# An expert mixture per unit of 128 tokens, and a rearranged beginning, in a fused linear-attention and mixture kernel

## The chip, the cores and the metric

The kernel runs on one core of a Trainium2 chip. The metric is the device time of one launch in microseconds (us), as the median of several launches. Engines: PE is TensorE (matmuls), PEld its loads of stationary operands, DVE is VectorE, ACT is ScalarE, POOL is GpSimd, SP is SyncE, which in this kernel does nothing but issue DMA transfers. L504 is line 504 of the kernel in question; the changed kernel has other line numbers than the one before.

## The reference, cut to what matters

```python
# attention: 4 batches, 8 heads, 768 steps, head size 40, float32
for t in range(S):
    y[:, :, t] = einsum('bhd,bhde->bhe', rt, state)
    Sa = einsum('bhde,bhe->bhd', state, at)
    state_decay = state * wt[:, :, None, :] - einsum('bhd,bhe->bhde', Sa, bt)
    state = state_decay + einsum('bhd,bhe->bhde', vt, kt)
# y becomes x: 3072 tokens of 320 values. Mixture of 4 experts, F = 1024:
for e in range(E):
    h = maximum(x @ w1[e], 0.0)
    out += p[:, e:e + 1] * (h @ w2[e])       # p: domain_probs, normalized per token
```

## The kernel before

The recurrence is done in 12 chunks of 64 steps. Two batches of a chunk make a unit of 128 tokens, so there are 24 units: 0 and 1 are the first chunk, 2 and 3 the second, and so on. For each unit the kernel loads six inputs (W, A, B, K, V, R) and then has four stages:

- `within`: everything that needs no state. TensorE transposes the inputs and multiplies them; VectorE copies the results through a causal mask (for instance the scores of V and R, into `CT`).
- `substitute`: a forward substitution in 31 steps of two instructions each, on VectorE for units 0 and 1 and on GpSimd for the others.
- `merge`: the substitution's result is turned into `Qc`, `QTc` and `QT`.
- `step`: state update and the unit's output, matmuls `py` on TensorE, `Y` on VectorE. Twelve small DMA transfers then rearrange Y to `xT`, the moving operand of the mixture.

The mixture is cut into pieces, and after each stage one piece is placed, so that TensorE has work while the chain of small operations waits. Python generators express this; a scheduler then settles the order on each engine, and each engine runs its instructions in that order.

```python
def mixture(c, xT):                    # c: a chunk, so 256 tokens = two units
    def up(e, quad):                   # half an expert: 16 + 8 matmuls of 256 columns
        for f in range(4):
            for g in range(2):
                nc.tensor.matmul(out=ph[f % 2][:, f // 2, :],
                    lhsT=w1_sb[:, e, g, (f0 + f) * P:(f0 + f + 1) * P], rhs=xT[:, g, :], ...)
        ...                            # w_last: rows 256 to 319 of w1, on half the array
        nc.scalar.activation(out=h[:], in_=ph[i][:], func=ACTF.Relu)
    def down(e, s):                    # one expert for one unit: 8 matmuls of 320 columns
        ...
# ... (order at the start)
load(0)                                # SyncE: inputs of unit 0
run(within(units[0]))
substitute(units[0], nc.vector)
load(1)
load_experts()                         # SyncE: gates and all weights
run(within(units[1]))
first_merge = merge(units[0]); run(first_merge, 2)
substitute(units[1], nc.vector)
for u in range(NU):
    ...
    load(u + 2)                        # SyncE
    ...
    if n == 6 and more:
        substitute(units[u + 2], nc.gpsimd)
    mix(1)                             # one piece of mixture
    if q.bp == B // 2 - 1:             # after every second unit
        work.append(mixture(q.c, xT))
```

## Time and profile before

| kernel before | |
|---|---|
| time, median of the first 3 launches | 1286.18 us (1285.4 to 1286.84) |
| profiled launch, span and mean granted clock | 1286.0 us, 0.965 |
| TensorE busy | 1201.8 us (93%) |
| first mixture matmul | 122.6 us |
| period of a unit in the steady part | 49.46 us |

The prediction below shows the lines of this profile and reads them: about 160 us at the beginning, and the full part behind them.

### The profile page before, as it was taken

What the parts mean: (1) busy time and instruction counts of PE and PEld (TensorE: products, weight loads), DVE (VectorE), ACT (ScalarE), POOL (GpSimd) and SP (SyncE); (2) the same over time, 40 slices, a digit from 0 to 9 for tenths busy, and PEclk for the clock granted to TensorE, in tenths of its full rate; (3) what the DMA queues carried; (4) which work ended last, traced back from release to release, by engine and by line L of the source; (5) the groups of instructions that cost most, each with busy time, mean ns of one, the idle gap of its engine ahead of it and who ended that gap; (6) DMA issues with size and microseconds to landing.
All of it is one profiled execution on the core that took longest, in us unless ns stands there. A gap on an engine that the chain in (4) does not pass through costs nothing.

```text
span 1286.0 us, 38173 instructions
## 1 busy us (share of the span) xinstructions
PE 1201.8 (93%) x16416; PEld 928.3 (72%) x16416; DVE 403.6 (31%) x854; ACT 320.8 (25%) x801; POOL 474.0 (37%) x1601
## 2 busy tenths in 40 slices
PE   4454799999999999999999999999999999999998
PEld 3443677777777777777777777777777777777776
DVE  6853223233143143143142232232331431411000
ACT  2121222232222222322222222232222222222111
POOL 2025632633534524525425426326335345240000
PEclk8656899999999999999999999999999999999999
DMA  4941111121120220220220220210211201000000
GB/s 63 319 71 26 29 31 31 23 36 21 30 39 14 37 39 12 39 39 10 41 38 10 42 35 10 44 31 11 47 22 19 47 16 27 14 13 2 17 1 11
DMA packets 182200, 45.27 MB, mean 35 GB/s; under 512 B 162576, under 2 KB 181008, under 8 KB 182032
## 3 DMA queue, kind: packets, MB, share of 16 engines
q1 hardware_dynamic: 182032, 42.83, 17.2%
q8 instruction: 130, 2.13, 0.7%
q14 instruction: 38, 0.31, 0.1%
HBM read 34.13 MB, written 3.93 MB: 30 GB/s over the span
## 4 chain that ended last, share of the span: by engine, by line
PE 88%; POOL 3%; ACT 2%; DVE 2%; SPq 2%; issue 2%; DMA 1%; DVEq 0%; ACTq 0%
PE po L505 33%; PE ph L487 26%; PE ph L493 8%; PE py L240 2%; PE psd L240 2%; SPq L157 2%; POOL Z L338 1%; POOL tmp L334 1%; PE pc L240 1%; PE pf L240 1%; PE psa L240 1%; PE px L240 1%; PE psn L240 1%; ACT QT L377 1%; PE pY L360 1%
## 5 line engine op out<-in xcount | busy, mean ns | idle before, releaser
L505 PE MATMUL po<-w_sb,hs 128*128 128x320 f32 x1536 | 441.9, 439 | 0.0
L505 PEld LDWEIGHTS po<-w_sb,hs 128*128 128x128 f32 x1536 | 282.5, 190 | 112.5 <-issue 3.6
L487 PE MATMUL ph<-xT,w_sb 128*128 128x256 f32 x1536 | 355.5, 384 | 0.0
L487 PEld LDWEIGHTS ph<-xT,w_sb 128*128 128x128 f32 x1536 | 286.3, 191 | 39.4 <-issue 0.3
L334 POOL TENSOR_TENSOR tmp<-M,Z 128x60 f32<-128x60 f32 (+24 forms) x682 | 188.7, 277 | 97.2 <-DVE M L327 45.5
L338 POOL TENSOR_TENSOR Z<-Z,tmp 128x60 f32<-128x60 f32 (+24 forms) x682 | 194.0, 285 | 53.4
L499 ACT ACTIVATE hs<-ph 128x512 f32<-128x512 f32 x192 | 104.3, 595 | 395.1 <-PE ph L493 395.1
L322 POOL COPY blocks<-F 32x256 f32<-32x256 f32 x88 | 34.7, 394 | 385.1 <-ACT F L303 382.4
L513 DVE SCALAR_TENSOR_TENSOR osb<-po,gate,osb 128x320 f32<-128x320 f32 x72 | 39.6, 551 | 249.9 <-PE po L505 249.9
L493 PE MATMUL ph<-xT,w_last 64*128 64x256 f32 x768 | 108.9, 402 | 0.0
L493 PEld LDWEIGHTS ph<-xT,w_last 64*128 64x128 f32 x768 | 66.1, 186 | 36.1 <-issue 31.8
L248 DVE COPY_PREDICATED TT<-mask_up,px 128x256 f32<-128x256 int32 x48 | 18.7, 438 | 192.2 <-PE px L240 192.2
L248 DVE COPY_PREDICATED TT<-mask_up,pe 128x256 f32<-128x256 int32 x48 | 18.6, 438 | 135.1 <-PE pe L240 135.1
L259 ACT COPY G<-pw 128x504 f32<-128x504 f32 x24 | 13.9, 580 | 188.5 <-DVE Y L461 150.8
L327 DVE STREAM_TRANSPOSE M<-blocks 128x1024 f32<-128x1024 f32 x24 | 46.8, 1951 | 33.0 <-POOL blocks L322 32.9
L330 POOL COPY Z<-unit_cols 128x256 f32<-128x256 f32 x22 | 8.8, 398 | 122.0 <-DVE Qc L345 122.0
L273 DVE RECIPROCAL gp<-gp 128x320 f32<-128x320 f32 x24 | 51.4, 2143 | 0.0
L315 ACT COPY EV<-pev 64x160 f32<-64x160 f32 x96 | 22.9, 286 | 101.1 <-PE pev L240 100.9
L353 POOL COPY QT<-QTc 32x256 f32<-32x256 f32 x96 | 40.1, 417 | 14.3 <-DVE QTc L347 7.6
L213 PE MATMUL pg<-ident,G 128*128 128x128 f32 x96 | 17.6, 311 | 29.2 <-DVE G L260 29.2
L511 DVE TENSOR_SCALAR osb<-po,gate 128x320 f32<-128x320 f32 x24 | 13.2, 551 | 91.1 <-PE po L505 91.1
L283 ACT COPY AT<-pAT 128x512 f32<-128x512 f32 x24 | 14.1, 586 | 107.9 <-PE pAT L213 107.9
(111 smaller groups left out, 1200.0 us busy)
## 6 DMA issues: line engine op xcount, KB each, us to landing
w_sb<-in_moe_w_dram SPq DMA_DIRECT2D x4, 1280.0 KB
w_sb<-in_moe_w_dram SPq DMA_DIRECT2D x8, 512.0 KB
natW<-in_w_dram SPq DMA_DIRECT2D x48, 80.0 KB
natA<-in_a_dram SPq DMA_DIRECT2D x48, 80.0 KB
natB<-in_b_dram SPq DMA_DIRECT2D x48, 80.0 KB
natK<-in_k_dram SPq DMA_DIRECT2D x48, 80.0 KB
out_dram<-osb SPq DMA_DIRECT2D x48, 80.0 KB
xT<-Y SPq DMA_DIRECT2D x168, 20.0 KB
```

Source lines behind the costliest of these rows:

```text
L240: nc.tensor.matmul(out=p[row][half(col), at * out_cols:(at + 1) * out_cols], lhsT=lhsT, rhs=rhs, start=(n == 0), stop=(n == len(terms) - 1),)
L248: nc.vector.copy_predicated(out=of_slot(m[:], s), mask=mask_up[:, None, :].to_broadcast([P, NJ, L]), data=p[s],)
L273: nc.vector.reciprocal(out=gp[:], in_=gp[:])
L327: nc.vector.transpose(out=M[:], in_=cols)
L334: eng.tensor_tensor(out=t, in0=M[:, j:j + 1, j + 1:Q].to_broadcast([P, n, m]), in1=Z[:, 0:n, j:j + 1].to_broadcast([P, n, m]), op=ALU.mult,)
L338: eng.tensor_tensor(out=Z[:, 0:n, j + 1:Q], in0=Z[:, 0:n, j + 1:Q], in1=t, op=ALU.add)
L353: ins = nc.gpsimd.tensor_copy(out=q.QT[quarter(i), :, quarter(i % 2)], in_=QTc[quarter(i)])
L487: nc.tensor.matmul(out=ph[f % 2][:, f // 2, :], lhsT=w1_sb[:, e, g, (f0 + f) * P:(f0 + f + 1) * P], rhs=xT[:, g, :], start=(g == 0 and f < ...
L493: nc.tensor.matmul(out=ph[i][:, f // 2, :], lhsT=w1_last[i * DT:(i + 1) * DT, e, (f0 + f) // 2, :], rhs=xT[i * DT:(i + 1) * DT, 2, :], sta ...
L499: nc.scalar.activation(out=h[:], in_=ph[i][:], func=ACTF.Relu)
L505: nc.tensor.matmul(out=po[:], lhsT=hs[e, f // 4, f % 2][:, f % 4 // 2, s * P:(s + 1) * P], rhs=w2_sb[:, e, f, :], start=(f == 0), stop=(f ...
L513: nc.vector.scalar_tensor_tensor(out=osb[s][:], in0=po[:], scalar=sc, in1=osb[s][:], op0=ALU.mult, op1=ALU.add,)
```

## The change

The diff says it in its title: the mixture works on one unit of 128 tokens, with whole experts as pieces; the first two units are interleaved; their loads are split over two queues; and the weights come through GpSimd's queue. Its intent is to give TensorE mixture work as soon as unit 0's output is there, instead of unit 1's, and to get that output sooner.

```diff
+    for u in range(2):
+        begin(u)
+    load(units[0], "V", nc.scalar)
+    for u, names in ((0, "WA"), (1, "W"), (0, "BK"), (1, "ABK"), (0, "R"), (1, "VR")):
+        load(units[u], names)
...
     def load_experts():
-                nc.sync.dma_start(out=gate..., w1_sb..., w1_last..., w2_sb...)
+                nc.gpsimd.dma_start(out=gate..., w1_sb..., w1_last..., w2_sb...)
...
-    def causal(m, p):
+    def causal(m, p, pinned=False):        # pinned: VectorE keeps these masked copies where
...                                         # they stand in the program (units 0 and 1)
-    def mixture(c, xT):
+    def mixture(q, xT):
-        def up(e, quad):                   # 16 matmuls of 256 columns
+        def up(e):                         # 32 matmuls of 128 columns
...
-    run(within(units[0])) ... substitute(units[0], nc.vector); load(1); load_experts() ...
+    load_experts()
+    ws = [within(units[u]) for u in range(2)]
+    for u in (0, 1, 0, 0, 1, 0):
+        next(ws[u])
+    z = substitute(units[0], nc.vector)    # now a generator: other work stands inside it
+    next(z)
+    for u in (1, 1, 0):                    # the 0 here: causal scores of unit 0
+        next(ws[u])
+    next(z)
+    run(ws[1])                             # and those of unit 1
+    run(z)
+    normalize()
...
+        if u == 0:
+            run(before)
+            run(substitute(units[1], nc.vector))
...
+            if n == 3:
+                work.append(mixture(q, xT))   # after every unit
```

(Not shown: second buffers for the inputs, smaller tiles, the order of the stages in the loop.)

More of the change, by code (lines that the diff above doesn't have):

```diff
@@ L61 @@
     NU = NC * B // 2
-    NTOK = 2 * P
     DT = DM - 2 * P
@@ L121 @@
     nat = {
-        x: kept(f"nat{x}", of_64, n, float(x == "W"), nc.vector, D) for x, n in (("W", 1), ("R", 1), ("V", 3))
+        x: kept(f"nat{x}", of_64, n, float(x == "W"), nc.vector, D) for x, n in (("W", 2), ("R", 2), ("V", 3))
     }
@@ L136, with begin @@
     units = []
-    def load(u):
+    def begin(u):
         q = Unit()
@@ L143, in load @@
         q.n = {}
-        for x in srcs:
+        units.append(q)
+        return q
+    def load(q, names, eng=nc.sync):
+        for x in names:
             if x in nat:
@@ L147, in load @@
             else:
-                t = sb.tile([P, H, D], FP32, name=f"nat{x}", tag=f"nat{x}")
+                t = sb.tile([P, H, D], FP32, name=f"nat{x}", tag=f"nat{x}", bufs=2)
             q.n[x] = t
@@ L156, in load @@
                 for o, h in parts:
-                    nc.sync.dma_start(out=to[:, o, :], in_=src[h].rearrange("h t e -> t h e"))
-        units.append(q)
-    load(0)
+                    eng.dma_start(out=to[:, o, :], in_=src[h].rearrange("h t e -> t h e"))
+    for u in range(2):
[3 more added lines that the diff above has]
+        load(units[u], names)
     w1_sb = const.tile([P, E, 2, F], FP32, name="w1_sb")
@@ L172, in load_experts @@
             for i in range(2):
-                nc.sync.dma_start(
+                nc.gpsimd.dma_start(
                     out=gate[i * L:(i + 1) * L, :, bp, :],
@@ L180, in load_experts, with normalize @@
             for g in range(2):
-                nc.sync.dma_start(out=w1_sb[:, e, g, :], in_=moe_w1[e, g * P:(g + 1) * P, :])
+                nc.gpsimd.dma_start(out=w1_sb[:, e, g, :], in_=moe_w1[e, g * P:(g + 1) * P, :])
             last = moe_w1[e, 2 * P:DM, :].rearrange("d (f two c) -> d f two c", two=2, c=P)
             for i in range(2):
-                nc.sync.dma_start(out=w1_last[i * DT:(i + 1) * DT, e], in_=last[:, :, i, :])
-            nc.sync.dma_start(out=w2_sb[:, e], in_=moe_w2[e].rearrange("(f p) d -> p f d", p=P))
-        nc.vector.reduce_sum(out=total[:], in_=gate[:], axis=AX.X)
+                nc.gpsimd.dma_start(out=w1_last[i * DT:(i + 1) * DT, e], in_=last[:, :, i, :])
+            nc.gpsimd.dma_start(out=w2_sb[:, e], in_=moe_w2[e].rearrange("(f p) d -> p f d", p=P))
+    def normalize():
+        tc.keep_in_program_order(nc.vector.reduce_sum(out=total[:], in_=gate[:], axis=AX.X))
         nc.vector.tensor_scalar_add(out=total[:], in0=total[:], scalar1=1e-9)
@@ L244, in quadrants @@
         return [by(x[:, 0:NJ * out_cols], out_cols) for x in p]
-    def causal(m, p):
+    def causal(m, p, pinned=False):
         for s in range(2):
-            nc.vector.copy_predicated(
+            ins = nc.vector.copy_predicated(
                 out=of_slot(m[:], s), mask=mask_up[:, None, :].to_broadcast([P, NJ, L]), data=p[s],
             )
+            if pinned:
+                tc.keep_in_program_order(ins)
         return m
@@ L284, in turned, with causal_scores @@
             return t
-        q.RT = turned("RT", n["R"], True)
-        VT = turned("VT", q.V)
-        q.CT = causal(CTs(), quadrants("pc", BY_TOKENS, L, lambda j, s, i: (
-            d_half(j, s), i, j, of_pairs(VT, d_half(j, s), j, i), of_pairs(q.RT, d_half(j, s), j, i),
-        )))
+        def causal_scores():
+            q.RT = turned("RT", n["R"], True)
+            VT = turned("VT", q.V)
+            q.CT = causal(CTs(), quadrants("pc", BY_TOKENS, L, lambda j, s, i: (
+                d_half(j, s), i, j, of_pairs(VT, d_half(j, s), j, i), of_pairs(q.RT, d_half(j, s), j, i),
+            )), q.start)
+        if not q.start:
+            causal_scores()
         yield
@@ L307, in within @@
         yield
+        if q.start:
+            causal_scores()
         q.EV = EVs()
@@ L322, in substitute @@
             ins = eng.tensor_copy(out=blocks[quarter(i)], in_=q.F[quarter(i), :, quarter(i % 2)])
-            if i == 0:
-                tc.keep_in_program_order(ins)
+            tc.keep_in_program_order(ins)
         M = sb.tile([P, Q, Q], FP32, name="M")
@@ L329, in substitute @@
         tmp = sb.tile([P, Q * Q // 8], FP32, name="tmp", tag="tmp", bufs=2)
-        eng.tensor_copy(out=Z[:], in_=unit_cols[:])
+        tc.keep_in_program_order(eng.tensor_copy(out=Z[:], in_=unit_cols[:]))
         for j in range(Q - 1):
@@ L338, in substitute @@
             eng.tensor_tensor(out=Z[:, 0:n, j + 1:Q], in0=Z[:, 0:n, j + 1:Q], in1=t, op=ALU.add)
+            if j in (3, 10):
+                yield
     def merge(q):
@@ L461, in step @@
             nc.vector.tensor_tensor(out=Y[:], in0=Y[:], in1=Gv, op=ALU.mult)
-        cols = slice(q.bp * P, (q.bp + 1) * P)
         for h in range(H):
@@ L470, in step @@
                     nc.sync.dma_start(
-                        out=xT[to:to + hi - lo, g, cols],
+                        out=xT[to:to + hi - lo, g, :],
                         in_=Y[at:at + hi - lo, h // 2].rearrange("p i t -> p (i t)"),
@@ L475, in step, with down @@
         yield
-    def mixture(c, xT):
-        osb = [sb.tile([P, DM], FP32, name="osb", tag="osb", bufs=4) for _ in range(2)]
-        def up(e, quad):
-            ph = [ps.tile([P, 2, NTOK], FP32, name="ph", tag="mm", bufs=4) for _ in range(2)]
-            f0 = 4 * quad
-            for f in range(4):
+    def mixture(q, xT):
+        osb = sb.tile([P, DM], FP32, name="osb", tag="osb", bufs=2)
+        hs = {}
+        def up(e):
+            ph = [ps.tile([P, NF // 2, P], FP32, name="ph", tag="mm", bufs=4) for _ in range(2)]
+            for f in range(NF):
                 for g in range(2):
                     nc.tensor.matmul(
-                        out=ph[f % 2][:, f // 2, :], lhsT=w1_sb[:, e, g, (f0 + f) * P:(f0 + f + 1) * P],
+                        out=ph[f % 2][:, f // 2, :], lhsT=w1_sb[:, e, g, f * P:(f + 1) * P],
                         rhs=xT[:, g, :], start=(g == 0 and f < 2), stop=False,
                     )
-            for f in range(0, 4, 2):
+            for f in range(0, NF, 2):
                 for i in range(2):
                     nc.tensor.matmul(
-                        out=ph[i][:, f // 2, :], lhsT=w1_last[i * DT:(i + 1) * DT, e, (f0 + f) // 2, :],
-                        rhs=xT[i * DT:(i + 1) * DT, 2, :], start=False, stop=(f == 2),
+                        out=ph[i][:, f // 2, :], lhsT=w1_last[i * DT:(i + 1) * DT, e, f // 2, :],
+                        rhs=xT[i * DT:(i + 1) * DT, 2, :], start=False, stop=(f == NF - 2),
                     )
             for i in range(2):
-                h = sb.tile([P, 2, NTOK], FP32, name="hs", tag="hs", bufs=6)
+                h = sb.tile([P, NF // 2, P], FP32, name="hs", tag="hs", bufs=6)
                 nc.scalar.activation(out=h[:], in_=ph[i][:], func=ACTF.Relu)
-                hs[e, quad, i] = h
-        def down(e, s):
+                hs[e, i] = h
+        def down(e):
             po = ps.tile([P, DM], FP32, name="po", tag="mm", bufs=4)
@@ L505, in down @@
                 nc.tensor.matmul(
-                    out=po[:], lhsT=hs[e, f // 4, f % 2][:, f % 4 // 2, s * P:(s + 1) * P], rhs=w2_sb[:, e, f, :],
+                    out=po[:], lhsT=hs[e, f % 2][:, f // 2, :], rhs=w2_sb[:, e, f, :],
                     start=(f == 0), stop=(f == NF - 1),
                 )
-            sc = gate[:, c, s, e:e + 1]
+            sc = gate[:, q.c, q.bp, e:e + 1]
             if e == 0:
-                nc.vector.tensor_scalar(out=osb[s][:], in0=po[:], scalar1=sc, scalar2=None, op0=ALU.mult)
+                nc.vector.tensor_scalar(out=osb[:], in0=po[:], scalar1=sc, scalar2=None, op0=ALU.mult)
             else:
                 nc.vector.scalar_tensor_tensor(
-                    out=osb[s][:], in0=po[:], scalar=sc, in1=osb[s][:], op0=ALU.mult, op1=ALU.add,
+                    out=osb[:], in0=po[:], scalar=sc, in1=osb[:], op0=ALU.mult, op1=ALU.add,
                 )
-        hs = {}
-        up(0, 0)
+        up(0)
         yield
         for e in range(E):
-            up(e, 1)
+            if e + 1 < E:
+                up(e + 1)
+                yield
+            down(e)
             yield
-            for s in range(2):
-                if s == 1 and e + 1 < E:
-                    up(e + 1, 0)
-                    yield
-                down(e, s)
-                yield
-        for s in range(2):
-            for i in range(2):
-                row = (2 * s + i) * S + c * L
-                nc.sync.dma_start(out=out[row:row + L, :], in_=osb[s][i * L:(i + 1) * L, :])
+        for i in range(2):
+            row = q.b[i] * S + q.c * L
+            nc.sync.dma_start(out=out[row:row + L, :], in_=osb[i * L:(i + 1) * L, :])
     work = []
@@ L548, in run @@
                 break
-    run(within(units[0]))
-    substitute(units[0], nc.vector)
-    load(1)
     load_experts()
-    run(within(units[1]))
-    first_merge = merge(units[0])
-    run(first_merge, 2)
-    substitute(units[1], nc.vector)
-    m = first_merge
+    ws = [within(units[u]) for u in range(2)]
[9 more added lines that the diff above has]
+    normalize()
+    m = merge(units[0])
+    run(m, 2)
     for u in range(NU):
         q = units[u]
-        if q.bp == 0:
-            xT = sb.tile([P, 3, NTOK], FP32, name="xT", tag="xT", bufs=2)
+        xT = sb.tile([P, 3, P], FP32, name="xT", tag="xT", bufs=3)
         s = step(q, xT)
@@ L568 @@
         if more:
-            load(u + 2)
+            load(begin(u + 2), srcs)
             w = within(units[u + 2])
-        for n, stages in enumerate(((before, s), (s,), (s,), (m, s, w), (w,), (w,), (w,), (w, m))):
+        for n, stages in enumerate(((before, s), (s,), (s,), (s, m, w), (w,), (w,), (w,), (w, m))):
             for gen in stages:
                 next(gen, None)
+            if n == 3:
+                work.append(mixture(q, xT))
             if n == 6 and more:
-                substitute(units[u + 2], nc.gpsimd)
-            mix(1)
-        if q.bp == B // 2 - 1:
-            work.append(mixture(q.c, xT))
+                run(substitute(units[u + 2], nc.gpsimd))
+            if u or n % 2:
+                mix(1)
     mix(-1)
```

## The prediction

> **What bounds the kernel now.** I read the page first, then the busy times by stretch, the chain of waits, and the timeline of single stages.
>
> ```profile
> PE 1201.8 (93%) x16416; PEld 928.3 (72%) x16416; DVE 403.6 (31%) x854; ACT 320.8 (25%) x801; POOL 474.0 (37%) x1601
> ...
> PE   4454799999999999999999999999999999999998
> ...
> PEclk8656899999999999999999999999999999999999
> ```
>
> TensorE is full from the sixth slice on. Everything before, about 160 us, is half empty and runs at a reduced granted clock. The stretches give numbers:
>
> ```profile
> 0.00:65.00 65.00, 30.20 (x600) 25.50 (x600) 48.56 (x155) 13.93 (x33) 9.73 (x36) 0.75 0.75 192
> 65.00:123.00 58.00, 25.37 (x503) 21.55 (x500) 24.89 (x64) 9.54 (x24) 24.75 (x76) 0.59 0.28 44
> 123.00:161.00 38.00, 31.28 (x576) 24.55 (x576) 10.00 (x22) 10.32 (x28) 20.93 (x71) 0.89 0.20 34
> 161.00:1286.00 1125.00, 1114.98 (x14748) 856.73 (x14744) 320.15 (x615) 287.01 (x717) 418.60 (x1418) 1.00 0.14 26
> ```
>
> (Columns: stretch, its length, busy us of PE, PEld, DVE, ACT, POOL, granted clock, DMA share, GB/s.) From 161 us PE is busy 1115 of 1125 us, so only two things can move the end: when dense work starts, and what the dense work costs.
>
> Why it starts late: the first mixture matmul needs a whole chunk of 256 tokens, so units 0 and 1. The output of unit 1 waits behind the substitution of unit 2, which runs on GpSimd, because VectorE executes in order:
>
> ```profile
> 113.45 0.61 DVE L345 STREAM_TRANSPOSE Qc<-Z 128x256 f32<-128x256 f32 x1 [14.37 <-POOL Z L338]
> 113.92 0.40 DVE L456 TENSOR_TENSOR Y<-py,G 128x256 f32<-128x256 f32 x1
> ...
> 116.94 1.12 PE L213 MATMUL pg<-ident,G 128*128 128x128 f32 x4 [17.57 <-DVE G L260]
> ...
> 122.56 1.91 PE L487 MATMUL ph<-xT,w_sb 128*128 128x256 f32 x4
> ```
>
> The mixture thus begins at 122.6 us and is starved again until about 160. What a mixture piece costs is read in the tail, where nothing else runs:
>
> ```profile
> 1232.36 3.62 PE L487 MATMUL ph<-xT,w_sb 128*128 128x256 f32 x16
> 1235.90 1.13 PE L493 MATMUL ph<-xT,w_last 64*128 64x256 f32 x8
> 1236.97 4.57 PE L505 MATMUL po<-w_sb,hs 128*128 128x320 f32 x16
> ```
>
> From start to start, the up piece takes 1236.97 − 1232.36 = 4.61 us, and the whole round of up and down 9.02 us (the next up starts at 1241.38). Sixteen matmuls of 256 columns take 3.54 us, less about 0.09 at the change of shape: 216 ns each, which is 256 × 2 clocks of 2.4 GHz plus 2.5 ns. Sixteen of 320 take 269 ns each.
>
> **What the Trainium skill says.** "TensorE: Matmul & The Clock Gate", LDWEIGHTS (loading the stationary operand): a load costs its number of columns over 1.2 GHz, 107 ns for 128. The same page, Back-to-back issue gap: spacing is set by load and matmul together, and is N/2.4 plus about 2.5 ns when the matmul binds. The trace agrees: 216 and 269 ns show the 2.5 ns with two passes' worth of clocks for float32, and the first matmul after a change of shape waits about 105 ns for its load. "SBUF — State Buffer", Who interferes with whom: DMAs issued by GpSimd can be starved of descriptors by two-port VectorE copies. No row of this trace shows it, as every DMA is issued by SyncE.
>
> **The change, part by part.**
>
> *1. Up pieces of 128 columns.* Now 3072 full-array matmuls of 128 columns and as many loads replace 1536 of 256, and the half-array ones double likewise. Pieces, ReLUs (192), evictions (96) and down matmuls stay the same in number. So 256 columns with one load become 128 columns with one load. The matmul side would need 128 × 2/2.4 + 2.5 = 109 ns, the load side at least 107. What happens when the load binds is visible in small matmuls of 40 columns with 64-column loads:
>
> ```profile
> 599.96 0.34 PE L240 MATMUL psd<-natV,k_tok 64*64 64x40 f32 x8
> 600.07 0.34 PE L240 MATMUL psd<-Sa,n_tok 64*64 64x40 f32 x8
> 600.19 0.34 PE L240 MATMUL psd<-natV,k_tok 64*64 64x40 f32 x7
> ```
>
> Four tiles run side by side, so 8 instructions are 2 per tile, and 0.23 us for 16 is 58 ns each. Forty columns would stream in 33 ns; a 64-column float32 load needs 53. So a load overlaps the matmul before it, and a load-bound stream goes at load time plus about 5 ns. Doubled: 107 + 5 = 112 ns. An expert's up piece then has 32 × 112 + 8 pairs × 112 = 4.48 us of stream against 16 × 216 + 4 × 216 = 4.32 before: +0.16 us. Over 96 pieces this is **+15 us**, all on the bound engine.
>
> *2. The beginning.* From the order of instructions of the changed kernel: TensorE does units 0 and 1 without R and V first; VectorE starts the substitution of unit 0, then that of unit 1, both bare of reciprocals and gate arithmetic; unit 0's output Y stands right behind unit 1's substitution; the first up matmul stands shortly behind unit 2's first transposes. Estimate from durations of the trace (an estimate throughout):
> - W of unit 0 lands at 4.8 us as now; two scans of 1.2, arithmetic and a reciprocal of 2.15 per unit, then blocks 1.2 and M 1.95: the first substitution starts near 25 us (now 27).
> - It is 62 steps at about 0.245 us = 15.2, plus six masked copies of other work at 0.35 each: done at 42.5; gate arithmetic, Qc and QTc to 44.5 (now 49.9).
> - blocks and M again: unit 1's substitution runs from 48, with 2 us of foreign work, to 65. Y follows at 65.8 (now 65.8 for unit 0, but 114.9 for the one that matters).
> - xT: 12 issues of about 0.74 us; eight suffice for the first matmuls. 6 us plus 1.15 us of landing: first up matmul at **73 us instead of 122.6**.
>
> From then on other work fills TensorE. To the end of unit 1's output: 4 up pieces × 4.78, 2 down × 4.50 and about 9 us of small matmuls, with 4 for cold clock and stalls: 41 us, hence unit 1 ends at 114.
>
> *3. Steady state.* The order keeps 8 pieces per unit and 6 between the substitution's input and its first use, as before; the unit period was 49.5 us (890.2 us for 18 units) and becomes 49.5 + 4 × 0.16 = 50.1. The nearest danger is xT: up now follows the output by two down pieces and transposes, about 12.8 us, where before it had five pieces. Eight of the twelve transfers landed 9.9 to 11.6 us after the output in the old trace, all twelve in 13.1 to 14.2, and the late ones are needed only 3.6 us into the piece. It fits, with 1 us to spare.
>
> *4. Double buffers, two queues, weights on GpSimd's queue.* These allow part 2 and have no worth of their own; the weights (needed from 73 us) took about 30 us at some 340 GB/s before.
>
> *Sum.* Unit 1 ends at 114. Then 20 units × 50.1 = 1002, the last two units 48.5 + 43.4 (47.9 and 42.8 before, plus 0.6 each), then 4 up and 6 down pieces = 46, and 4 us for the last transfer: 114 + 1002 + 92 + 50 = **1258 us**. I say 1257. Undivided, the beginning alone would give about 1242.
>
> **The rivals.** (a) *Weight loads bind harder.* The same skill section gives 81 ns for sustained 128-column bfloat16 pairs, 25 above its streaming formula; 25 ns more per load here would be +40 × 22 ns × 96 = +85 us, so about 1340, slower. Against it: full-array transposes of 128 columns run at 109 ns now (though with a cheaper load), and the 58 ns above. (b) *The load is hidden fully*, 109 ns: 1247. (c) *xT comes late in every unit*: each us costs 24, so 2 us late gives about 1300, no gain. (d) *The beginning gains less*: GpSimd's queue holds 24 DMAs ahead of its QT copies, and weights compete with the first inputs; 10 us lost gives 1267. For it: DMA is saturated at 40 to 60 us now. Against: QT is needed only near 48 us and has 8 us of slack, since Y waits for VectorE anyway.
>
> **Range and chances.** The beginning is good to ±7 us, the load-bound spacing to −3/+5 ns (−11/+19 us). I take 1243 to 1278. Faster by over 2% means below 1260.5, just beyond my value: 0.54. Within 2%: 0.41. Slower needs rival (a) or a bad (c): 0.05.
>
> **What would show it.** Right: up pieces near 4.78 us in the tail; first up matmul near 73 us; PE over 98% busy from there; unit period near 50.1 us. Part 1 is wrong if up matmuls of 128 columns start 109 or over 116 ns apart; part 2 if Y of unit 0 comes much off 66 us; part 3 if PE idles before the up pieces of each unit, released by xT.

## The result, and the profile after

The changed kernel took 1270.85 us (median of 4, 1269.48 to 1272.12), beside 1286.51 us for the kernel before in the same rounds: a ratio of 0.9879, with a 95% interval of 0.9862 to 0.9896. That is 1.2% faster, inside the predicted range, 14 us above the predicted 1257, and "the same" by the 2% line, to which the prediction gave 0.41, against 0.54 for "faster". Ratios here and below are the mean time of one kernel's fast runs over the mean of the other's of the same rounds, so they are not quite the ratio of the quoted medians.

The page of the changed kernel, with TensorE's busy time, and the slices of the span for TensorE and its granted clock:

```profile
PE 1201.4 (95%) x18720; PEld 1014.5 (80%) x18720; DVE 394.9 (31%) x856; ACT 320.1 (25%) x801; POOL 503.9 (40%) x1625
...
PE   3249999999999999999999999999999999999998
PEclk9559999999999999999999999999999999999999
```

The number of matmuls grew by 2304, as the halved up matmuls require, and the busy time did not move. TensorE is now full from the fourth slice on, where it was the sixth. The busy times by stretch (columns as in the prediction) show the same:

```profile
0.00:65.00 65.00, 20.67 (x312) 16.73 (x312) 29.82 (x95) 11.50 (x25) 23.85 (x55) 0.70 0.84 207
65.00:123.00 58.00, 41.33 (x738) 36.01 (x739) 32.22 (x108) 13.03 (x34) 13.80 (x41) 0.77 0.23 39
123.00:161.00 38.00, 38.00 (x547) 32.06 (x546) 13.56 (x26) 8.58 (x20) 17.41 (x58) 1.00 0.21 38
161.00:1269.00 1108.00, 1101.41 (x17127) 929.74 (x17125) 319.25 (x628) 287.01 (x722) 448.83 (x1473) 1.00 0.14 26
```

The second and third stretch are fuller than before. The first is emptier: VectorE, on which the first substitution runs, was busy for 29.8 us there instead of 48.6. Something holds up the beginning. The timeline of VectorE and of TensorE in that stretch (start in us, duration, engine, line, operation, and in brackets the idle time before it and what ended it):

```profile
25.39 0.49 DVE L288 TENSOR_TENSOR k_tok<-natK,gp 128x320 f32<-128x320 f32 x1 [3.29 <-DMA natK<-in_k_dram]
44.28 0.77 DVE L256 COPY_PREDICATED CT<-mask_up,pc 128x256 f32<-128x256 int32 x2 [11.12 <-PE pc L248]
57.84 0.77 DVE L256 COPY_PREDICATED CT<-mask_up,pc 128x256 f32<-128x256 int32 x2 [9.31 <-PE pc L248]
68.06 0.60 DVE L363 STREAM_TRANSPOSE Qc<-Z 128x256 f32<-128x256 f32 x1
88.83 0.75 DVE L474 TENSOR_TENSOR Y<-py,G 128x256 f32<-128x256 f32 x2
89.50 0.61 DVE L363 STREAM_TRANSPOSE Qc<-Z 128x256 f32<-128x256 f32 x1
```

```profile
35.98 0.66 PE L221 MATMUL pRT<-ident,natR 128*128 128x128 f32 x2 [7.17 <-DMA natR<-in_r_dram]
40.81 0.66 PE L221 MATMUL pRT<-ident,natR 128*128 128x128 f32 x2 [4.17 <-DMA natR<-in_r_dram]
53.95 1.09 PE L221 MATMUL pRT<-ident,natR 128*128 128x128 f32 x4 [8.95 <-DMA natR<-in_r_dram]
95.75 0.71 PE L504 MATMUL ph<-xT,w_sb 128*128 128x128 f32 x4
```

Read the first block from the top. VectorE stands still three times, for 3.3 us just ahead of unit 0's substitution (whose steps run from 29.8 us) and for 11.1 and 9.3 us inside it. Each time it has reached an instruction of *other* work that stands in its order: the product with unit 1's K, and the two pairs of masked copies CT of units 0 and 1. The second block says why the copies were not ready: TensorE waited for R to land, for unit 0 until 36 and 41 us, for unit 1 until 54. R of unit 1 was also issued late: SyncE needed 16.5 us for the six issues of unit 1's V ahead of it (3.9 us in e2 below) and was through with R at 52.0 us. Unit 0's Qc came at 68 us and its Y at 88.8, right ahead of unit 1's Qc (the last line of the first block), and the first mixture matmul at 95.8.

The tail, where nothing else runs, gives the cost of a piece:

```profile
1242.13 3.73 PE L504 MATMUL ph<-xT,w_sb 128*128 128x128 f32 x32
1245.80 1.16 PE L510 MATMUL ph<-xT,w_last 64*128 64x128 f32 x16
1246.89 4.57 PE L522 MATMUL po<-w_sb,hs 128*128 128x320 f32 x16
1251.30 3.73 PE L504 MATMUL ph<-xT,w_sb 128*128 128x128 f32 x32
```

From start to start the up piece takes 4.76 us (before: 4.61) and the round of up and down 9.17 (before: 9.02). The period of a unit is 49.74 us, from the ends of the output matmuls of unit 1 (133.62) and unit 21 (1128.35) divided by 20; before it was 49.46.

### The profile page after: what moved, and what is told of

The parts are those of the page before. It is cut to its first block, busy times and chain, and to the rows that moved or that the text cites. A ratio compares the mean times of both kernels' runs of the same rounds, so it can differ in the third digit from the quotient of the medians.

```text
span 1269.1 us, 42660 instructions
## 1 busy us (share of the span) xinstructions
PE 1201.4 (95%) x18720; PEld 1014.5 (80%) x18720; DVE 394.9 (31%) x856; ACT 320.1 (25%) x801; POOL 503.9 (40%) x1625
## 3 DMA queue, kind: packets, MB, share of 16 engines
q1 hardware_dynamic: 170288, 32.13, 14.4%
## 4 chain that ended last, share of the span: by engine, by line
PE 91%; DMA 4%; DVE 2%; ACT 1%; SPq 1%; issue 0%; DVEq 0%; ACTq 0%
PE po L522 34%; PE ph L504 28%; PE ph L510 8%; PE py L248 2%; PE psd L248 2%; DMA natV<-in_v_dram 2%; ACT QT L395 1%; PE pc L248 1%; PE psn L248 1%; PE pQ L390 1%; PE px L248 1%; PE psa L248 1%; PE pY L378 1%; PE pf L248 1%; PE pev L248 1%; DMA natK<-in_k_dram 1%
## 5 line engine op out<-in xcount | busy, mean ns | idle before, releaser
L504 PE MATMUL ph<-xT,w_sb 128*128 128x128 f32 x3072 | 366.0, 277 | 0.0
L504 PEld LDWEIGHTS ph<-xT,w_sb 128*128 128x128 f32 x3072 | 350.7, 192 | 5.4
L371 POOL COPY QT<-QTc 32x256 f32<-32x256 f32 x96 | 54.8, 571 | 208.8 <-DVE QTc L365 205.0
L510 PE MATMUL ph<-xT,w_last 64*128 64x128 f32 x1536 | 111.6, 285 | 0.0
L510 PEld LDWEIGHTS ph<-xT,w_last 64*128 64x128 f32 x1536 | 93.2, 187 | 11.6
L450 ACT COPY RS<-prs 64x256 f32<-64x256 f32 x88 | 32.3, 367 | 103.2 <-PE prs L248 102.1
L464 DVE TENSOR_TENSOR state<-psd,state 128x160 f32<-128x160 f32 x44 | 12.3, 319 | 117.9 <-PE psd L248 117.9
L293 ACT COPY RT<-pRT 128x512 f32<-128x512 f32 x24 | 14.1, 586 | 101.9 <-PE pRT L221 101.9
L395 ACT COPY QT<-pQ 32x256 f32<-32x256 f32 x48 | 17.4, 363 | 85.5 <-PE pQ L390 85.2
L248 PE MATMUL py<-CT,k_tok 64*64 64x64 f32 x768 | 29.9, 230 | 7.9 <-DVE TT L256 7.9
```

Source lines behind the costliest of these rows:

```text
L248: nc.tensor.matmul(out=p[row][half(col), at * out_cols:(at + 1) * out_cols], lhsT=lhsT, rhs=rhs, start=(n == 0), stop=(n == len(terms) - 1),)
L371: ins = nc.gpsimd.tensor_copy(out=q.QT[quarter(i), :, quarter(i % 2)], in_=QTc[quarter(i)])
L504: nc.tensor.matmul(out=ph[f % 2][:, f // 2, :], lhsT=w1_sb[:, e, g, f * P:(f + 1) * P], rhs=xT[:, g, :], start=(g == 0 and f < 2), stop=False,
L510: nc.tensor.matmul(out=ph[i][:, f // 2, :], lhsT=w1_last[i * DT:(i + 1) * DT, e, f // 2, :], rhs=xT[i * DT:(i + 1) * DT, 2, :], start=Fals ...
```

## The experiments

**T1**: the weights, issued by GpSimd from 8.7 us on, share the DMA engines with the inputs of units 0 and 1. R and K come late, and the copies that stand in VectorE's order turn that into about 24 us of stalls (3.3 + 11.1 + 9.3), which reach the first up matmul. **T2**, a rival: the inputs are late by SyncE's own pace, and the weights do not matter. **T3**, a rival: the lateness does not matter, since without it another wait takes over. A separate question is whether the up matmuls are bound by their loads.

In the table "out 1" and "out 2" are the ends of the last output matmul (py) of units 1 and 2, in the profiled launch. The last column is that launch's span less "out 2". The runs came in several groups; the kernel before, run beside each, had medians from 1286.51 to 1287.83 us, so differences of a microsecond between groups mean nothing.

| kernel | first up matmul | out 1 | out 2 | time (median) | ratio to before | span − out 2 |
|---|---|---|---|---|---|---|
| changed kernel | 95.8 | 133.6 | 183.3 | 1270.9 | 0.9879 | 1085.8 |
| e1 weights wait | 86.0 | 125.9 | 175.7 | 1262.2 | 0.9807 | 1085.7 |
| e2 weights on SyncE | 80.6 | 120.8 | 170.5 | 1258.6 | 0.9781 | 1085.8 |
| e3 scores later | 85.3 | 125.0 | 174.8 | 1261.7 | 0.9806 | 1085.6 |
| e8 xT on ScalarE | 65.2 | 114.1 | 169.6 | 1255.4 | 0.9751 | 1085.6 |
| e7 unit 2's loads later | 64.8 | 110.8 | 165.8 | 1253.7 | 0.9734 | 1085.8 |
| e9 and its substitution on VectorE | 64.1 | 109.2 | 159.1 | 1247.7 | 0.9695 | 1085.6 |
| e4 mixture alone | 83.5 | 123.3 | 173.0 | 1260.7 | 0.9791 | 1085.6 |
| e10 e4, loads later | 70.8 | 117.4 | 172.0 | 1259.4 | 0.9782 | 1085.7 |
| e12 e10, substitution on VectorE | 71.3 | 117.9 | 167.6 | 1254.8 | 0.9748 | 1085.6 |

The last column is the table's main reading. With the mixture in units of 128 tokens, every one of these kernels needs 1085.7 ± 0.1 us after unit 2's output. All that separates them is when that output comes. So each experiment is about the first 185 us, and a gain that does not reach "out 2" is no gain.

### e1: the weights wait for the first inputs

Ahead of the 24 weight and gate transfers, 18 tiny GpSimd copies that read unit 1's R write into every destination, so no weight transfer starts before the last input has landed.

```diff
+    last_in = units[1].n["R"][:, :, 0:1].rearrange("p h o -> p (h o)")
+    for touched in [...]:                  # a corner of every weight and gate destination
+        nc.gpsimd.tensor_copy(out=touched, in_=last_in[:, 0:touched.shape[-1]])
     load_experts()
```

> The changed kernel, with every weight and gate transfer held back until the last input of units 0 and 1 has landed (tiny GpSimd copies from unit 1's R into each destination; TensorE's and VectorE's instructions stand in the same order). T1 (the weights' traffic delays R and K of units 0 and 1, and the pinned masked copies turn that into stalls of 11.1 + 9.3 + 3.3 us inside unit 0's substitution): R of unit 0 is transposed near 18 to 22 us instead of 36 to 41, the stalls of VectorE before its masked copies fall under 3 us together, Y of unit 0 comes near 67 instead of 88.8, the first up matmul near 75 instead of 95.8, and the total falls by about 20 us, to 1247 to 1252. T2 (the loads are late by the Sync queue's own pace, whatever the weights do): R stays near 36, the time at 1270 within 4 us. T3 (the early inputs arrive, but another wait takes over, as weights that now come late): first up matmul stays after 88 us and the gain is under 10 us; PE would be seen waiting for w1 or w2.

Measured: 1262.15 us, 8.7 less than the changed kernel. The cause that T1 names was right: R of unit 0 was transposed at 24.2 us, VectorE waited no more than 0.2 us for the masked copies inside unit 0's substitution, and Qc came at 43.7 (about 43 by the prediction's working) instead of 68. But only 9 of the 24 us reached the end, and the total missed T1's range. Two waits took over. GpSimd, busy with issuing the delayed weights, was late with QT, and TensorE waited 11.7 us for it:

```profile
59.56 0.69 PE L248 MATMUL psa<-QT,EV 64*64 64x64 f32 x6 [11.67 <-POOL QT L371]
```

And unit 0's output, complete at 70 us, was handed on only from 81.6, behind inputs of later units on SyncE. So T2 fell, and T3 is half true: other waits took over, though TensorE did not wait for weights.

### e2: the weights on SyncE, behind the first inputs

```diff
-                nc.gpsimd.dma_start(out=w1_sb[:, e, g, :], ...)      # and all other weights
+                nc.sync.dma_start(out=w1_sb[:, e, g, :], ...)
```

> The changed kernel, with the weight and gate transfers issued by SyncE behind the inputs of units 0 and 1, as the kernel before had them behind its own. T1: the same as holding them back, R of unit 0 near 18 to 22 us, total 1247 to 1252; if some weights overlap the last inputs of unit 1 then up to 1256. T2: 1270 within 4 us. T3: the gain is under 10 us, and the first up matmul waits for weights.

Measured: 1258.58 us, 12.3 less than the changed kernel, outside both T1's 1247 to 1252 (1256 with some overlap) and T2's 1270. The busy times by stretches of 10 us show the traffic; the last two columns are the share of the DMA engines and GB/s. First the changed kernel, then e2:

```profile
10.00:20.00 10.00, 6.21 (x84) 5.13 (x82) 6.78 (x11) 2.73 (x6) 7.69 (x13) 1.00 1.06 208
20.00:30.00 10.00, 4.20 (x89) 3.19 (x80) 6.56 (x13) 2.61 (x6) 4.31 (x7) 0.81 1.04 307
```

```profile
10.00:20.00 10.00, 6.21 (x82) 5.19 (x80) 7.21 (x11) 2.51 (x6) 0.00 (x0) 1.00 0.49 77
20.00:30.00 10.00, 6.44 (x159) 5.17 (x155) 9.51 (x30) 4.33 (x11) 0.00 (x0) 1.00 0.35 36
```

The inputs alone kept the DMA engines busy for 0.49 and 0.35 of these stretches; with the weights beside them the share is over 1 from 10 us on. The Trainium skill says it in "DMA: Bandwidth & Descriptors", section "Issuing engines are not separate DMA queues": whichever engine issues them, DMAs run on the same 16 DMA engines and interleave, and more queues save only issue time. These rows agree, with 1.06 against 0.49 of the engines in the same 10 us. In e2 unit 0's Qc comes when the prediction's working had it, and then this happens (the timelines of TensorE and VectorE, then of SyncE's queue):

```profile
24.36 0.68 PE L221 MATMUL pRT<-ident,natR 128*128 128x128 f32 x4
43.41 0.61 DVE L363 STREAM_TRANSPOSE Qc<-Z 128x256 f32<-128x256 f32 x1
58.06 0.42 DVE L474 TENSOR_TENSOR Y<-py,G 128x256 f32<-128x256 f32 x1 [1.02 <-PE py L248]
65.93 0.62 DVE L363 STREAM_TRANSPOSE Qc<-Z 128x256 f32<-128x256 f32 x1
```

```profile
52.11 7.73 SPq L160 DMA_DIRECT2D natW<-in_w_dram  x2
...
71.41 3.91 SPq L160 DMA_DIRECT2D natR<-in_r_dram  x6
75.42 9.01 SPq L487 DMA_DIRECT2D xT<-Y  x12
```

Unit 0's Y was there at 58.1 us, 31 us earlier than in the changed kernel. Only 24.7 of these were gained by Qc (43.4 instead of 68.1). The other 6 come from an order that the scheduler settled anew: in e2, e7, e8 and e9 Y stands in the midst of unit 1's substitution (unit 1's Qc follows 7.9 us later), in the changed kernel and in e1 behind its last step. So the expectation of e1, that VectorE's order stays the same, does not hold for all of these edits, and what this order is worth was not tested alone. In e2 it gave nothing to the first up matmul, because the transfers of Y to xT waited for SyncE. They left at 75.4, and the first up matmul followed at 80.6. Until then SyncE issued the inputs of unit 2, which stand ahead in its order. These 20 issues (the expectations below say 18) took 23.2 us here, with the weights in flight, where they take 13.8 us in e7 later on. In the changed kernel the inputs of units 2 and 3 were through by 82 us, before the late Y came, so this wait was hidden. It is a new theory, **T4**: SyncE's order took the place of the wait removed. Its rival **T5**: the weights or unit 2's inputs hold the first up matmul whatever SyncE's order is.

### e3: the causal scores after the substitution

The loads stay as late as in the changed kernel; only the pinned masked copies leave the substitution.

```diff
-        if q.start:
-            causal_scores()
+        q.scores = causal_scores
...
     normalize()
+    units[0].scores()
...
             run(substitute(units[1], nc.vector))
+            units[1].scores()
```

> The changed kernel with weights and loads as they are, but the first two units' causal scores (transposes of R and V, their matmuls and the two pinned masked copies) are moved behind the substitution of their unit. Loads stay late (R of unit 0 at 36 to 41 us). T1: VectorE no longer stands still inside unit 0's substitution, of the 24 us of stalls only K's 3.3 and part of R's remain; Qc of unit 0 near 48 instead of 68, first up matmul near 76 to 80, total 1250 to 1256. If the order of VectorE is not what turns the late R into lost time (T2 with another wait), the total stays at 1266 to 1272.

Measured: 1261.74 us, 9.1 less than the changed kernel. The stalls inside the substitution went, but TensorE, in its order, still stood ahead of unit 0's R. It waited for unit 1's V, whose last part came at 49 us:

```profile
49.16 0.66 PE L248 MATMUL pev<-natV,TT 64*64 64x40 f32 x14 [2.79 <-DMA natV<-in_v_dram]
```

So VectorE stood once for 11.4 us ahead of the masked copies, and Qc came at 54.3, where I had expected 48. Y of unit 0 came at 77.6, and the first up matmul at 85.3, after T1's 76 to 80: SyncE's loads ended at 80.8 and the transfers left at 80.9. The total lies between the two expected ranges. The order on VectorE does turn lateness into lost time, though moving the copies removes only part of the loss.

### e6: narrower up matmuls

```diff
-                        out=ph[f % 2][:, f // 2, :], ..., rhs=xT[:, g, :], ...
+                        out=ph[f % 2][:, f // 2, 0:96], ..., rhs=xT[:, g, 0:96], ...
```

> Wrong result on purpose: the up matmuls stream 96 columns instead of 128, with the same 128-column weight loads and the same number of instructions. If the load binds (as the prediction said: 107 ns of load plus about 5), the up piece in the tail keeps its 4.76 us and the spacing of full-array up matmuls its 111.7 ns. If the matmul binds, the spacing falls to about 96*2/2.4 + 2.5 = 82.5 ns and the piece to about 3.6 us, and the whole to about 1270 - 96 * 1.1 = 1165 us.

One launch: 1267.56 us. Its result is wrong, as intended. The tail:

```profile
1239.00 3.71 PE L506 MATMUL ph<-xT,w_sb 128*128 128x96 f32 x32
1242.64 1.14 PE L512 MATMUL ph<-xT,w_last 64*128 64x96 f32 x16
1243.71 4.58 PE L524 MATMUL po<-w_sb,hs 128*128 128x320 f32 x16
```

The 32 matmuls take 3.64 us from start to start of the next group, with 128 columns 3.67, and the piece 4.71 against 4.76. A quarter of the streaming was taken away and 1% of the time went with it. So streaming does not bind. That it is the load, and not some other cost of each instruction, was not tested by a shorter load; it is inferred from the measured 112 ns beside the 58 ns at which the prediction's small matmuls ran with 64-column loads.

### e7 and e8: two ways around SyncE's order

Both start from e2. In e7 the inputs of unit 2 are loaded behind unit 0's output transfers; in e8 unit 0's twelve transfers are issued by ScalarE.

```diff
 e7:
-            load(begin(u + 2), srcs)
+            begin(u + 2)
+            if u:
+                load(units[u + 2], srcs)
...
+                if u == 0 and n == 3 and gen is m:    # right behind unit 0's step
+                    load(units[2], srcs)
 e8:
-                    nc.sync.dma_start(out=xT[...], ...)
+                    (nc.sync if q.u else nc.scalar).dma_start(out=xT[...], ...)
```

> The kernel of e2_weights_sync with the 18 input loads of unit 2 standing behind unit 0's output transfers on SyncE instead of ahead of them; every queue keeps its kind of work. T4: the transfers go out at about 59.5, first up matmul near 67 to 70, but unit 2's W now lands near 71 instead of 66, and its R and V near 80 to 82, so unit 1's output comes within 3 us of e8's, total 1244 to 1252. T5: total stays at 1254 to 1259.

> The kernel of e2_weights_sync (weights on SyncE behind the first inputs), with the twelve transfers of unit 0's output to xT issued by ScalarE instead of SyncE. In e2 unit 0's output was ready at 58.1 us, but its transfers were issued from 75.4, right behind the 18 input loads of unit 2, which stand ahead of them on SyncE and were stretched by the weights (52 to 75 us). T4 (SyncE's order is the wait that took the place of the one removed): the transfers go out at about 59 to 60, the first up matmul comes near 67 to 70 instead of 80.5, the output of unit 1 near 107 to 111 instead of 120.8, total 1244 to 1249. T5 (the weights themselves hold the first up matmul, or unit 2's inputs hold TensorE): the first up matmul stays after 76 and the total at 1254 to 1259.

Measured: e7 1253.69 us, e8 1255.37. T4 held at its own place: the transfers went out 1.0 us after the output, and the first up matmul came at 64.8 and 65.2, earlier than the prediction's 73. (The prediction had Y behind unit 1's substitution; with Y there, at about 66, the first up matmul of e7 would have come near 72, an estimate from e7's Y at 58.3 and unit 1's Qc at 66.1.) "Out 1" came at 110.8 and 114.1, where the prediction had 114. The totals did not follow: e7's lies between the ranges of T4 and T5, and e8's in T5's (why e8 is 3 us behind e7 at "out 1" was not followed up). For e7, of the 10 us by which "out 1" was earlier than in e2, only about 5 are left at "out 2". VectorE of e7 there:

```profile
110.95 0.74 DVE L474 TENSOR_TENSOR Y<-py,G 128x256 f32<-128x256 f32 x2
116.80 0.61 DVE L363 STREAM_TRANSPOSE Qc<-Z 128x256 f32<-128x256 f32 x1 [5.12 <-POOL Z L354]
```

Unit 2's substitution runs on GpSimd, and VectorE waits 5.1 us for it; TensorE then stands for 3.4 us, ahead of the transposes of unit 3's gates. This is **T6**, the next wait. **T7**: moving it to VectorE only makes VectorE late for other things.

### e9: unit 2's substitution on VectorE

```diff
-                run(substitute(units[u + 2], nc.gpsimd))
+                run(substitute(units[u + 2], nc.gpsimd if u else nc.vector))
```

> The kernel of e7_load2_later with unit 2's substitution on VectorE instead of GpSimd. In e7 unit 1's output came at 110.8 us, but unit 2's Q, whose substitution ran on GpSimd from 94.7 us on, only at 116.8, and the step from unit 1's output to unit 2's took 54.97 us instead of the usual 49.73. T6 (this is the next wait): VectorE finishes it before unit 1's output, that step falls to 49.7 to 51, and the total to 1247 to 1250. T7 (VectorE then holds up evictions and masked copies, so that TensorE waits for those instead): total within 2 us of e7's 1253.7.

```profile
109.85 0.75 DVE L474 TENSOR_TENSOR Y<-py,G 128x256 f32<-128x256 f32 x2
110.51 0.62 DVE L363 STREAM_TRANSPOSE Qc<-Z 128x256 f32<-128x256 f32 x1
```

Measured: 1247.74 us (1246.49 to 1249.48), ratio 0.9695 (0.9679 to 0.9711). Qc of unit 2 follows unit 1's Y at once, and the step from "out 1" to "out 2" is 49.9 us. T6 holds. The result is correct, and the kernel beats both the kernel before, by 3.0%, and the changed one.

### e4 and e5: each half of the change alone

e4 keeps the old beginning, loads and weights, and takes only the mixture per unit of 128 tokens. e5 takes the new beginning, loads and weights, and keeps the mixture of 256 tokens.

```diff
 e4, against the kernel before:
-        if q.bp == 0: xT = sb.tile([P, 3, NTOK], ...)      # and mixture(c, xT) per chunk
+        xT = sb.tile([P, 3, P], ...)                       # and mixture(q, xT) per unit
 e5, against the changed kernel: the same lines the other way round
```

> Part 1 alone: beginning and loads as in the kernel before, mixture per unit of 128 tokens. Estimate from the trace of before: unit 0's output at 65 us is followed by its transfers, so the first up matmul comes near 78, and unit 0's eight pieces (37 us) fill TensorE's gaps up to unit 1's output at 114 to 120, instead of starting at 122.6; against it stand 24 units * 0.27 us = 6.5 us of longer period. If most of the change's gain is in the finer mixture, the total is 1255 to 1268; if unit 1's substitution behind unit 2's (14.4 us of waiting for GpSimd) still decides, 1268 to 1280.

> Part 2 alone: the changed beginning and loads, mixture in chunks of 256 tokens with half experts as pieces, as before. The first up matmul needs units 0 and 1; in the changed kernel unit 1's Q is done at 89.5 us, so without mixture between, its output comes near 105 to 110, the first up near 116 instead of 122.6, and the period falls back to 49.46 us. Estimate: 1274 to 1284. If the early start is worth something by itself, without the finer pieces, the total falls under 1270.

Measured: e4 1260.72 us, which is 27.1 less than the kernel before in its rounds (1287.83); e5 1299.72, which is 11.9 more. Their sum, −15.2, is the −15.7 of the whole change within what the medians allow. So the whole gain comes from the mixture per unit, and the rearranged beginning, as it stands in the change, costs 10 us (changed kernel against e4: 1270.9 against 1260.7). The estimate for e5, 1274 to 1284, was wrong. In e5 the first up matmul needs unit 1's output. Its matmuls ended at 109.2 us, as estimated, but VectorE did its Y at 125.2 only, behind

```profile
124.74 0.62 DVE L364 STREAM_TRANSPOSE Qc<-Z 128x256 f32<-128x256 f32 x1 [15.46 <-POOL Z L355]
```

which is the wait for GpSimd that already held up the kernel before (14.4 us there).

### e11: the new beginning alone, with the weights on SyncE

The edit is e2's, applied to e5.

```diff
-                nc.gpsimd.dma_start(out=w1_sb[:, e, g, :], ...)      # and all other weights
+                nc.sync.dma_start(out=w1_sb[:, e, g, :], ...)
```

> The kernel of e5_prologue_alone (changed beginning, mixture of 256 tokens; 1299.7 us, 12 more than the kernel before) with weights issued by SyncE behind the first inputs. T1: the 12 us are the weights' traffic on GpSimd's queue; unit 0's Q comes near 43.5 instead of 66, everything of the beginning some 20 us earlier, total 1274 to 1284, at or below the kernel before. Rival: the interleaving of two units itself costs the time, total stays at 1292 to 1300.

Measured: 1284.95 us, just above T1's range, ratio 0.9989 (0.9968 to 1.001). Moving the weights is worth 14.8 us here, and Qc of unit 0 came at 43.5. T1's weights account for the 12 us that e5 lost. What remains of the new beginning is worth nothing measurable with the coarse mixture, because VectorE waits 14.7 us for GpSimd's substitution of unit 2 before it does unit 1's Y.

### e10 and e12: the old beginning, with the same two repairs

e10 is e4 with e7's edit, and e12 is e10 with e9's.

```diff
 e10:
-        if more:
-            load(u + 2)
+        if more and u:
+            load(u + 2)
...
+                if u == 0 and n == 3 and gen is m:    # right behind unit 0's step
+                    load(2)
 e12, besides:
-                substitute(units[u + 2], nc.gpsimd)
+                substitute(units[u + 2], nc.gpsimd if u else nc.vector)
```

> The kernel of e4_mixture_alone (old beginning, finer mixture) with unit 2's input loads behind unit 0's output transfers on SyncE, the edit of e7. In e4 the output of unit 0 ended at 65.7, its transfers went out 12.6 us later, first up matmul at 83.5, unit 1's output at 123.3. If the same SyncE wait decides here, the first up matmul comes near 73 to 76 and unit 1's output near 113 to 117; a wait of up to 5 us for GpSimd's substitution of unit 2 may follow, as in e7: total 1251 to 1257. If the loads of unit 2 then come too late for the old beginning, it stays at 1259 to 1263.

> The kernel of e10_old_start_load2 (old beginning, finer mixture, unit 2's loads behind unit 0's transfers) with unit 2's substitution on VectorE, the edit of e9. In e10 unit 1's output came at 117.4 us, and the step to unit 2's took 54.6 instead of 49.7, with 5.1 us of VectorE waiting for GpSimd. T6 (the wait for GpSimd ate the gain of e10): the step falls to 49.7 to 51 and the total to 1252 to 1256. T7 (VectorE's load makes a new wait): 1258 to 1261. Beside e9 (1247.7), T6 also tells what interleaving units 0 and 1 is worth when the weights do not disturb it: 5 to 8 us, about the 8.2 us by which unit 1's output is earlier there.

Measured: e10 1259.44 us, only 1.3 less than e4 and above the 1251 to 1257 expected. "Out 1" came 5.9 us earlier, just beyond the expected range, but VectorE waited 5.1 us for GpSimd in the next step, so "out 2" was 1.0 us earlier. I had named that wait and not subtracted it fully. e12: 1254.76 us, as T6 expected; its step from "out 1" to "out 2" is 49.7 us. e10 gained almost nothing because its gain ran into the next wait. Beside e9 (1247.74), e12 also tells what the interleaved beginning is worth once nothing disturbs it: 7.0 us by the medians, 8.5 by "out 2".

## Why the prediction was right or wrong

By its own steps:

1. *Up pieces of 128 columns.* Right: 4.76 us measured for the up piece, where the working gave 4.61 + 0.16. e6 shows that streaming does not set the 112 ns; that the load does is inferred, not tested alone. Rival (a), 25 ns more per load, did not happen.

2. *The beginning.* This is the step that failed. "First up matmul at 73 us" was 95.8, and "unit 1 ends at 114" was 133.6, so 19.6 us late. The chain itself was about right: from the first up matmul to unit 1's end 37.9 us (predicted 41), and without the weights' traffic Qc of unit 0 came at 43.7 and 43.4 (predicted about 43). What failed is the sentence in part 4 that the queues "have no worth of their own", with weights "needed from 73 us". I asked when the weights are needed, and not what they displace while they land. Rival (d) did name that "weights compete with the first inputs", and gave 1267; it was set aside because QT has slack. But the traffic did not bite through QT. It bit through K and R and the masked copies that wait for R, which the change pins inside unit 0's substitution. e1, e2 and e3 show both links.

   There was a second error in it, which the lateness covered up. I let unit 0's transfers leave as soon as Y was there. e2 shows that SyncE had the 20 loads of unit 2 ahead of them. The trace of the kernel before shows it too and could have been asked: there Y of unit 0 stands at 65.8 us, and its transfers leave at 78.2, behind the same loads. And e7 shows a third wait, for GpSimd, behind that. e2, the kernel without the disturbance, comes to within 2 us of the predicted 1257 only because errors cancel: its first up matmul at 80.6 instead of 73, against a cheaper steady part.

   The gain was also put down to the wrong half. The prediction credits it to "the beginning" as one thing. By e4 and e5, the mixture per unit brings all of it, even with the old beginning, since unit 0 alone then gives TensorE work, and the rearranged beginning takes 10 us back. So part 1 was no mere cost of 15 us, and "undivided, the beginning alone would give about 1242" stands against the 1299.7 of e5, and the 1285.0 of e11, where the weights do not disturb it.

3. *Steady state.* "50.1 us" was measured as 49.74, which is 0.28 us per unit above the kernel before instead of 0.64. The up pieces did grow as predicted: by the spacing of the matmuls in the trace they cost 0.68 us more per unit. The down matmuls (0.20) and two groups of small ones (psn 0.16 and pg 0.06) gave back 0.42 us. The prediction counted the mixture's up matmuls alone. The share of psn is idle time ahead of it that shrank: 4.9 us in 18 units before, mostly for QT from ScalarE, and 2.3 us in 20 units after. What made the other two cheaper was not tested and stays open. Over 20 units the time was 7.3 us under the predicted 1002. Rival (c), a late xT in every unit, did not happen: from unit 1 to unit 20 the first eight transfers had landed about 9.8 to 11.0 us after the output, and TensorE did not wait for them.

4. *Sum.* 133.6 instead of 114 (+19.6), 20 units in 994.7 us instead of 1002 (−7.3), the last two units and the tail in 140.8 instead of 142 (−1.2): 1258 + 19.6 − 7.3 − 1.2 gives the profiled span of 1269.1. With the error of the beginning alone it would be about 1278, the upper end of the range. So it was partly luck that the time fell well inside: an error of the other sign in the steady part helped. The signs that the prediction named for its own failure worked: "Y of unit 0 comes much off 66 us" (88.8), with up pieces near 4.78.

## What to carry to other kernels

A transfer that is not needed for a long time is not harmless. Ask what it shares while it lands, and follow the delayed data to the first in-order engine that stands still for it. When a wait is removed, list what stands next in each in-order queue (here SyncE's loads, then GpSimd's substitution) before counting the gain, because e10 removed 5.9 us and kept 1. In a kernel with a saturated steady part, find the point after which all versions take equally long (here unit 2's output, 1085.7 us ahead of the end) and judge each change by that point alone.

## What the Trainium skill lacked or had wrong

- "TensorE: Matmul & The Clock Gate", Back-to-back issue gap, gives about 81 ns for sustained pairs of 128 columns. It names no type there (bfloat16 is the prediction's word) and has no figure for float32. Here 32 float32 pairs of 128 columns with a full-array load took 3.67 us, about 112 ns each without the change of shape at the start, and with 96 columns 3.64. The section LDWEIGHTS of the same page, 107 ns for 128 columns, is the one that fits, with about 5 ns added.
- "DMA: Bandwidth & Descriptors", "Issuing engines are not separate DMA queues", is right (1.06 of the DMA engines' time with the weights beside the inputs, 0.49 without), but it calls issue time "usually small relative to the DMA itself". For small transfers it is not: twelve transfers to xT took 9.0 us to issue on one queue, and 20 input loads 23 us while the weights were in flight. That an issue queue holds back later and urgent transfers is the cost that mattered here, and the section does not name it.
- No page that I looked up says how much a small transfer is delayed by large ones in flight. Here R of unit 0, issued by 20 us in the changed kernel, was usable at 36 to 41 us with the weights in flight, and at 24 us at the latest in e2, where its issues ended at 16.7.
